# A new static step order for a chunked recurrent attention with an MLP: ones first on VectorE, some constants early, pads later

## The chip, the cores and the metric

One core of a Trainium2 chip. The metric is the time of one execution in microseconds (us). The kernel before took 266.17 us (median of three runs, 264.39 to 269.71). PE is TensorE, DVE is VectorE, ACT is ScalarE, POOL is GpSimd, SP is SyncE, which here only issues DMA.

## The reference, cut to what matters

A recurrent attention (4 batches, 8 heads, 768 steps, head size 40), whose output goes through an MLP with a squared ReLU (3072 tokens, 320 to 2048 to 320):

```python
for t in range(S):
    y[:, :, t] = einsum('bhd,bhde->bhe', rt, state)
    Sa = einsum('bhde,bhe->bhd', state, at)
    state = state * wt[:, :, None, :] - einsum('bhd,bhe->bhde', Sa, bt)
    state = state + einsum('bhd,bhe->bhde', vt, kt)
...
h = x @ w_in
g = maximum(h, 0)**2
return g @ w_out
```

## The kernel before

The recurrence is worked in chunks of 64 steps. There are 24 groups (12 chunks of two pairs of batches), and each group runs the same list of some sixty named steps. A list in the source gives one order for all steps of all groups; each engine runs its own steps of it in that order. `KBS1.2` is step KBS1 of group 2; `~3` is three warm-up matmuls on a tile of ones.

```python
ORDER = """
TBL.0 zK2.0 LWb.0 zL1.0 zR1.0 zS2.0 LWa.0 zV3.0 zR2.0 zU0.0 LKa.0 LWa.1 ...
... (cut)
"""
class Plan:
    def add(self, name, g, eng, dur, fn, deps=(), mode=None, alloc=None, frees=None, dma=None):
        ...   # keeps name, group, engine, function, deps; dur and dma are not kept
    def run(self):
        for t in ORDER.split(): ...   # checks the deps, gives out PSUM buffers, returns the functions in that order
...
def load(name, dst, step, src, other, deps):     # four buffers for each kind
    eng = "ACT" if g == 0 and name in ("LK", "LB") else "POOL" if g >= AQ and name == "LA" else "SP"
    for be in range(2): ... q_.dma_start(out=..., in_=tok(src, b0 + be))
    ...
load("LW", wf, 0, w, False, lambda be: [("LN", g - NL)])
load("LK", kbf, 320, k, True, lambda be: [(f"KBS{be}", g - NL)])
load("LB", kbf, 320, b, False, lambda be: [(f"KBS{be}", g - NL)])
...
add("LN", g, "ACT", 0.47, f, [..., ("LWa", g), ("LWb", g), ...])
add(f"KBS{be}", g, *(("DVE", 0.47) if g < 3 and be else ("POOL", 0.87)), f, [..., ("LK" + "ab"[be], g), ("LB" + "ab"[be], g), ("EXN", g), ...])
...   # from group 6 on KB is transposed by a DMA in SyncE's queue:
add("KX", g, "SP", 1.25, f, [("KBS0", g), ("KBS1", g), ("EB", g - NK)], dma=(40, 0.036, 0.1 + late, 1.0))
...   # the output's store, also in SyncE's queue
add("OST", g, "SP", 0.6, f, [("OE", g)], dma=(5, 0.088, 1.15, 0.9))
```

The chain of a group is: LW (load of w, SyncE), LN (its logarithm, ACT), LO (GpSimd), CS and CE (cumulative sums, PE), exponentials (ACT), KBS (GpSimd; VectorE for the first three groups' second half) and AS (GpSimd), then transposes and matmuls. SyncE's queue holds the loads of w, k and b (but for k and b of group 0, which ACT issues), the first loads of a, the transposes KX and the stores OST, 190 entries in one file: an entry that waits holds up all behind it. From the sixth on each also waits on one of eight semaphores in turn (in the trace of the kernel before 23 to 25 entries are on each), so that at most eight are under way. GpSimd issues the loads of v and r, and those of a from group 4 on, between its own computing.

Of the kernel before, what the change touches and what calls it, by code (L numbers as in the profile page):

```python
# [8 lines left out]
BF16 = mybir.dt.bfloat16  # L9
# [6 lines left out]
TBL.0 zK2.0 LWb.0 zL1.0 zR1.0 zS2.0 LWa.0 zV3.0 zR2.0 zU0.0 LKa.0 LWa.1 zA1.0 zS1.0 LKb.0 LWa.2 zF1.0 LBa.0 ones.0  # L16
zV1.0 UI.0 LAa.0 zF0.0 UE.0 LBb.0 ID.0 LWb.1 zL0.0 zF2.0 LN.0 LV1.0 SELB.0 LKb.1 TI.0 LO.0 zK0.0 LAb.0 zA0.0 zS0.0
LV0.0 ~10 CS.0 TE.0 LWb.2 zR0.0 EXN.0 I2.0 CE.0 LR.0 LAb.1 KBS1.0 KBS0.0 EXE.0 LAb.2 LN.1 zV0.0 ~3 KT.0 LR.1 LBa.1
AS.0 KTE.0 SEL.0 ~3 AT.0 wi1.0 LAa.1 MASK.0 LN.2 ATE.0 GLM.0 VC.0 LO.1 ~2 EB.0 LBb.1 EBE.0 LV0.1 ~1 CE.1 LKa.1 LO.2
EXE.1 zU1.0 LWb.3 ~1 XV.0 zK1.0 RT.0 LR.2 UB.0 zF3.0 LAa.2 LV1.1 UA.0 zV2.0 RTE.0 ~2 COR.0 wi2.0 CS.1 MA.0 LWa.3  # L20
CE.2 AS.1 MB.0 EXN.1 LKb.2 LV1.2 ~1 AT.1 VT.0 EXE.2 LAa.3 ATE.1 wj1.0 VTE.0 ST.0 KBS0.1 KBS1.1 CP.0 zR3.0 LBa.2
LV0.2 CPE.0 KT.1 LBb.2 wj2.0 LN.3 KTE.1 LKa.2 AS.2 ~2 CS.2 RT.1 EXN.2 STE.0 LAb.3 YC.0 wj0.0 RTE.1 EB.1 YE.0 LO.3
SX.0 VC.1 EBE.1 LKa.3 LR.3 CE.3 wi0.0 EXE.3 SXE.0 XV.1 LBa.3 LV1.3 wp0.0 AT.2 UA.1 RT.2 ATE.2 LKb.3 UB.1 KBS0.2 CS.3
wp1.0 RTE.2 COR.1 KBS1.2 LBb.3 XT.0 AS.3 MA.1 KT.2 XTE.0 MB.1 U1.0 wo0.0 KTE.2 EXN.3 VT.1 LV0.3 AT.3 VC.2 VTE.1 EB.2
UX1.0 GLM.1 GLM.2 EBE.2 UY1.0 LWb.4 ST.1 RL1.0 KBS0.3 LWa.4 STE.1 XV.2 X0.2 CP.1 LBb.4 UB.2 GLM.3 U0.0 CPE.1 KBS1.3
UA.2 UY0.0 LWa.5 UX0.0 wo1.0 KT.3 RL0.0 ATE.3 COR.2 KTE.3 YC.1 MA.2 YE.1 RT.3 MB.2 EB.3 SQ0.0 SX.1 RTE.3 LWb.5 XT.1
VT.2 XTE.1 LN.4 LKb.4 D0.0 EBE.3 VC.3 LO.4 ST.2 U0.1 LV0.4 SXE.1 CS.4 SQ1.0 D1.0 EXN.4 LAa.4 LBa.4 UX0.1 STE.2 LR.4
UY0.1 CE.4 VTE.2 RL0.1 LKa.4 XV.3 X0.3 CP.2 LWa.6 LN.5 U1.1 CPE.2 KBS1.4 UY1.1 EXE.4 LWa.7 UX1.1 UB.3 LAb.4 SX.2
LKb.5 RL1.1 SQ0.1 D2.0 LV1.4 SXE.2 D3.0 LWb.8 UA.3 LO.5 YC.2 OE.0 YS.2 LWb.6 KBS0.4 COR.3 YE.2 RT.4 LBa.7 D0.1 SQ1.1
RTE.4 LR.5 KT.4 LWb.7 MA.3 LV1.5 XT.2 D1.1 MB.3 XTE.2 AS.4 KTE.4 ST.3 LKa.5 VC.4 CS.5 LAb.5 U1.2 LBa.5 AT.4 LN.6  # L30
LAa.5 UX1.2 ATE.4 LBb.5 EXN.5 VT.3 LR.6 UY1.2 VTE.3 LV0.6 EB.4 RL1.2 OST.0 CE.5 EBE.4 LO.6 D2.1 LKa.7 EXE.5 LV0.5
RT.5 LN.7 STE.3 LBb.6 XV.4 KBS0.5 X0.4 U0.2 UB.4 CP.3 UA.4 D3.1 LAa.6 CPE.3 UX0.2 LKb.6 OE.1 KBS1.5 UY0.2 RTE.5
SQ1.2 SX.3 LAb.6 RL0.2 KT.5 LKa.6 SXE.3 CS.6 GLM.4 KTE.5 LBa.6 LO.7 COR.4 EXN.6 YC.3 SQ0.2 YS.3 LWa.8 AS.5 RT.6 MA.4
CS.7 YE.3 RTE.6 OST.1 D0.2 LV1.6 EXN.7 AT.5 XT.3 LWa.9 LV1.7 D1.2 ATE.5 VC.5 XTE.3 KBS1.6 EB.5 LKb.7 U0.3 MB.4 EBE.5
CE.6 LR.7 LWb.9 VT.4 LN.8 KBS0.6 D2.2 VTE.4 EXE.6 LBb.8 XV.5 LAa.7 X0.5 CP.4 UA.5 AS.6 D3.2 CPE.4 LBb.7 UB.5 UY0.3
OE.2 LO.8 KX.6 AT.6 VC.6 UX0.3 ATE.6 GLM.5 ST.4 LAb.7 RL0.3 YC.4 LKb.8 YS.4 LAb.8 COR.5 YE.4 CS.8 MA.5 LV1.8 U1.3
SQ0.3 LKa.9 MB.5 XT.4 UX1.3 KBS0.7 EXN.8 STE.4 UY1.3 VT.5 OST.2 LAa.8 RL1.3 XTE.4 D0.3 LWb.10 VTE.5 KBS1.7 EB.6
LBa.9 U0.4 SQ1.3 CE.7 LR.8 EBE.6 UY0.4 LN.9 LKb.9 UX0.4 EXE.7 LAb.9 D1.3 RL0.4 LWa.10 LO.9 SX.4 CP.5 SXE.4 GLM.6
ST.5 LV0.7 CPE.5 KX.7 RT.7 XV.6 AS.7 X0.6 D2.3 UA.6 SQ0.4 LV0.9 LKa.8 UB.6 D3.3 RTE.7 STE.5 U1.4 LR.9 LBa.8 CS.9
OE.3 LV1.9 COR.6 YC.5 MA.6 YS.5 LV0.8 UY1.4 YE.5 MB.6 UX1.4 KBS1.8 LKb.11 XT.5 SX.5 RL1.4 XTE.5 LKb.10 AT.7 SXE.5  # L40
CE.8 OST.3 SQ1.4 D0.4 EXE.8 VT.6 EXN.9 ATE.7 D1.4 LBb.9 LN.10 ST.6 VC.7 LO.10 LKa.11 U0.5 STE.6 EB.7 KBS0.8 LWb.11
UX0.5 EBE.7 D2.4 GLM.7 UY0.5 LAa.9 D3.4 VTE.6 RL0.5 KX.8 AS.8 RT.8 XV.7 LV0.10 X0.7 OE.4 SQ0.5 CP.6 U1.5 UA.7 OST.4
UY1.5 CPE.6 RTE.8 LWa.11 UX1.5 UB.7 AT.8 D0.5 RL1.5 ATE.8 SX.6 CS.10 SXE.6 LBb.12 YC.6 EXN.10 SQ1.5 COR.7 LWa.12
KBS0.9 YS.6 RT.9 MA.7 YE.6 D1.5 LWb.12 RTE.9 LAa.10 XT.6 D2.5 LBa.10 VC.8 XTE.6 KBS1.9 EB.8 MB.7 U0.6 EBE.8 LKa.10
LR.10 UY0.6 VT.7 GLM.8 LBb.10 LV1.10 UX0.6 VTE.7 D3.5 RL0.6 CE.9 KX.9 XV.8 OE.5 SQ0.6 X0.8 ST.7 EXE.9 CP.7 LN.11
STE.7 AS.9 OST.5 U1.6 UA.8 UY1.6 CPE.7 UB.8 LAb.10 UX1.6 LBb.11 D0.6 RL1.6 LO.11 AT.9 SX.7 ATE.9 LAb.11 LBa.11 CS.11
SQ1.6 LV1.11 YC.7 LWa.13 COR.8 YS.7 LV0.11 MA.8 D1.6 LWb.13 YE.7 MB.8 D2.6 LR.11 EXN.11 LWa.14 XT.7 KBS0.10 CE.10
XTE.7 VC.9 SXE.7 EB.9 U0.7 KBS1.10 EXE.10 EBE.9 ST.8 VC.10 VT.8 LAa.11 KX.10 UY0.7 LN.12 STE.8 D3.6 LV0.12 VTE.8
UX0.7 OE.6 AS.10 LWb.14 SX.8 RL0.7 RT.10 OST.6 SXE.8 LO.12 XV.9 X0.9 CP.8 UA.9 GLM.10 U1.7 LV1.12 CPE.8 RTE.10 UY1.7
UX1.7 LKb.14 UB.9 AT.10 RL1.7 LKb.12 CS.12 ATE.10 YC.8 SQ0.7 COR.9 LKa.12 KBS1.11 YS.8 RT.11 MA.9 YE.8 LBa.12 D0.7  # L50
EXN.12 KBS0.11 SQ1.7 XT.8 D1.7 MB.9 XTE.8 LAa.12 EB.10 LKb.13 VC.12 U0.8 EBE.10 GLM.9 UY0.8 LR.12 RTE.11 KX.11 UX0.8
CE.11 VT.9 LN.13 LBb.14 D2.7 VTE.9 EXE.11 LO.13 XV.10 RL0.8 LBb.13 X0.10 AS.11 ST.9 CP.9 STE.9 VC.11 U1.8 LAb.13
D3.7 UA.10 CPE.9 LAb.12 UY1.8 UB.10 SX.9 OE.7 LR.13 UX1.8 SQ0.8 OST.7 CS.13 RL1.8 LKa.14 SXE.9 YC.9 YS.9 COR.10
KBS1.12 LKa.13 YE.9 EXN.13 AT.11 D0.8 ATE.11 KBS0.12 MA.10 CE.12 XT.9 D1.8 LN.14 LAa.13 XTE.9 MB.10 SQ1.8 EB.11
LO.14 U0.9 EXE.12 UY0.9 EBE.11 KX.12 GLM.11 VT.10 LV1.13 UX0.9 LR.14 VTE.10 ST.10 LWa.15 AS.12 XV.11 STE.10 X0.11
LWa.16 CP.10 UB.11 D2.8 CPE.10 UA.11 AT.12 RL0.9 D3.8 LWb.15 COR.11 ATE.12 RT.12 LBa.13 MA.11 YC.10 YS.10 MB.11 U1.9
YE.10 CS.14 LKa.15 OE.8 SQ0.9 SX.10 EXN.14 OST.8 XT.10 UY1.9 XTE.10 UX1.9 LBa.15 VT.11 RL1.9 LBa.14 D0.9 KBS0.13
VTE.11 EB.12 LKa.16 U0.10 SQ1.9 LAa.14 CE.13 EBE.12 D1.9 LAb.14 EXE.13 LKb.15 UY0.10 LN.15 LV0.13 LWb.16 UX0.10
RTE.12 SXE.10 D2.9 KBS1.13 RL0.10 ST.11 AS.13 KX.13 XV.12 STE.11 X0.12 CP.11 UA.12 GLM.12 U1.10 LV0.15 CPE.11 D3.9
LBb.15 AT.13 LV1.14 OE.9 UY1.10 UB.12 ATE.13 UX1.10 OST.9 LO.15 SQ0.10 RT.13 RL1.10 COR.12 YC.11 LWb.18 YS.11  # L60
KBS0.14 CS.15 YE.11 RTE.13 D0.10 LWa.17 EXN.15 LAa.15 XT.11 SX.11 LBa.16 XTE.11 MA.12 KBS1.14 EB.13 U0.11 MB.12
EBE.13 CE.14 LV0.14 LWb.17 D1.10 LN.16 LAb.15 VT.12 SQ1.10 EXE.14 KX.14 UX0.11 VC.13 LO.16 VTE.12 UY0.11 LV1.15
D2.10 SXE.11 LKb.17 RL0.11 XV.13 AS.14 RT.14 LBb.16 ST.12 LR.15 X0.13 STE.12 U1.11 UA.13 CP.12 LR.16 UB.13 UY1.11
# [80 lines left out]
def kernel(  # L144
# [21 lines left out]

# [526 lines left out]
```

## Time and profile before

| | before |
|---|---|
| median of 3 | 266.17 us |
| span of the profiled run, mean granted clock | 264.9 us, 0.988 |
| PE busy | 92% |
| PE late against its pace (see the prediction) at 39 us / at the end | 20.7 / 27.3 us |

The prediction below shows the page, the sums by stretch and the start. The lines of the waits: who waited for what, us in total, times, longest.

```profile
POOL KB L331 <- DMA KBf<-in_b_dram: 6.9, 3, 5.0
ACT LNW L282 <- DMA Wf<-in_w_dram: 3.4, 1, 3.4
```

GpSimd's wait of 5.0 us (at 129 us) cost PE little: the only stop of PE near it is 0.9 us at 139 us, for the transpose of that KB.

### The profile page before, as it was taken

What the parts mean: (1) busy time and instruction counts of PE and PEld (TensorE: products, weight loads), DVE (VectorE), ACT (ScalarE), POOL (GpSimd) and SP (SyncE); (2) the same over time, 40 slices, a digit from 0 to 9 for tenths busy, and PEclk for the clock granted to TensorE, in tenths of its full rate; (3) what the DMA queues carried; (4) which work ended last, traced back from release to release, by engine and by line L of the source; (5) the groups of instructions that cost most, each with busy time, mean ns of one, the idle gap of its engine ahead of it and who ended that gap; (6) DMA issues with size and microseconds to landing.
All of it is one profiled execution on the core that took longest, in us unless ns stands there. A gap on an engine that the chain in (4) does not pass through costs nothing.

```text
span 264.9 us, 13096 instructions
## 1 busy us (share of the span) xinstructions
PE 243.5 (92%) x5809; PEld 193.8 (73%) x5809; DVE 180.1 (68%) x296; ACT 163.2 (62%) x289; POOL 162.3 (61%) x244
## 2 busy tenths in 40 slices
PE   4887979999999999999999999999999899999970
PEld 1345767877877788787877788888878688878750
DVE  7659976696856676768666668686767658786520
ACT  2344665687755757775675876578485675646340
POOL 3789728987975469567489758576967593400000
PEclk9979999999999999999999999999999999999997
DMA  7999999798799699789699879779899677200110
GB/s 117 156 180 169 202 199 167 137 155 155 141 143 136 127 132 161 145 141 144 106 135 152 169 120 169 131 133 139 138 113 142 110 131 102 66 25 16 32 36 26
DMA packets 111913, 33.75 MB, mean 127 GB/s; under 512 B 101232, under 2 KB 109808, under 8 KB 111856
## 3 DMA queue, kind: packets, MB, share of 16 engines
q1 hardware_dynamic: 100272, 20.79, 52.0%
q0 software_dynamic: 9472, 11.80, 25.2%
q8 instruction: 45, 0.74, 1.2%
q10 hardware_dynamic: 2112, 0.33, 0.8%
q14 instruction: 12, 0.10, 0.1%
HBM read 28.84 MB, written 3.93 MB: 124 GB/s over the span
## 4 chain that ended last, share of the span: by engine, by line
PE 74%; DMA 5%; ACT 2%; issue 2%; POOL 1%; DVE 0%; ACTq 0%; POOLq 0%
PE fo L569 19%; PE hp L551 15%; DMA KBT<-KB 5%; PE hp L542 4%; PE vt L488 4%; PE sx L476 3%; PE eb L405 2%; PE cs L298 2%; PE x L420 2%; PE cp L405 2%; PE y L502 2%; PE ce L311 2%; PE rt L376 2%; PE st L457 2%; PE x L442 2%; PE ar L369 2%
## 5 line engine op out<-in xcount | busy, mean ns | idle before, releaser
L556 ACT ACTIVATE RL<-hp 128x1024 bf16<-128x1024 f32 x46 | 47.1, 1023 | 32.7 <-PE hp L551 32.2
L569 PE MATMUL fo<-WOUT,GT 128*128 128x320 bf16 x384 | 65.5, 300 | 0.6 <-DVE GT L560 0.5
L331 POOL TENSOR_TENSOR KB<-KBf,EXN 128x320 bf16<-128x320 f32 x45 | 40.6, 909 | 36.9 <-PE y L502 21.4
L551 PE MATMUL hp<-XT,WIN 128*128 128x128 bf16 x736 | 51.7, 219 | 1.1 <-issue 1.0
L551 PEld LDWEIGHTS <-WIN 128*128 128x128 bf16 x768 | 44.9, 98 | 4.8 <-issue 1.7
L560 DVE TENSOR_TENSOR GT<-RL 128x1024 bf16<-128x1024 bf16 x48 | 37.8, 787 | 9.0 <-ACT RL L556 8.9
L569 PEld LDWEIGHTS <-GT 128*128 128x128 bf16 x384 | 33.0, 98 | 11.9 <-DVE GT L560 1.1
L409 DVE TENSOR_TENSOR CPM<-cp,MASK 128x1024 bf16<-128x1024 f32 x24 | 29.3, 1220 | 8.5 <-PE cp L405 8.5
L409 DVE TENSOR_TENSOR EBM<-eb,MASK 128x1024 bf16<-128x1024 f32 x24 | 29.3, 1221 | 7.6 <-PE eb L405 7.4
L343 POOL DMA_DIRECT2D Vf<-in_v_dram x48 | 33.9, 706 | 0.0
L290 POOL TENSOR_TENSOR LLO<-LNW 128x320 bf16<-128x320 f32 x24 | 18.4, 767 | 19.5 <-ACT LNW L282 15.2
L264 POOL DMA_DIRECT2D Af<-in_a_dram x40 | 28.2, 706 | 0.4 <-issue 0.4
L433 ACT ACTIVATE UZ<-x 64x320 bf16<-64x320 f32 x48 | 20.7, 431 | 9.7 <-PE x L428 8.1
L337 POOL TENSOR_TENSOR A<-Af,EXE 128x320 bf16<-128x320 f32 x24 | 21.2, 882 | 6.8 <-ACT EXE L320 2.3
L447 ACT ACTIVATE VM<-x 64x320 bf16<-64x320 f32 x48 | 20.6, 430 | 7.6 <-PE x L442 6.8
L304 ACT ACTIVATE EXN<-cs 128x640 f32<-128x640 f32 x24 | 16.9, 702 | 10.4 <-PE cs L298 8.7
L468 DVE TENSOR_TENSOR STB<-st,GLM 128x640 bf16<-128x640 f32 x22 | 18.0, 818 | 7.7 <-PE st L462 7.1
L515 DVE TENSOR_TENSOR YB<-y,EXE 128x320 bf16<-128x320 f32 x24 | 11.8, 490 | 13.5 <-PE y L510 12.0
L492 DVE COPY VMT<-vt 128x1024 bf16<-128x1024 bf16 x24 | 16.5, 686 | 4.4 <-PE vt L488 4.3
L282 ACT ACTIVATE LNW<-Wf 128x320 f32<-128x320 f32 x24 | 11.2, 468 | 12.8 <-PE ce L315 7.0
L542 PE MATMUL hp<-XT,WIN 64*128 64x128 bf16 x368 | 18.1, 217 | 0.0
L347 ACT ACTIVATE VM<-Vf 128x640 bf16<-128x640 f32 x24 | 17.5, 732 | 0.3 <-DMA Vf<-in_v_dram 0.2
(90 smaller groups left out, 454.6 us busy)
## 6 DMA issues: line engine op xcount, KB each, us to landing
Wf<-in_w_dram SPq DMA_DIRECT2D x48, 80.0 KB
Vf<-in_v_dram POOLq DMA_DIRECT2D x48, 80.0 KB, 5.2
out_dram<-OSB SPq DMA_DIRECT2D x24, 160.0 KB
KBf<-in_k_dram SPq DMA_DIRECT2D x46, 80.0 KB
KBf<-in_b_dram SPq DMA_DIRECT2D x46, 80.0 KB
Af<-in_a_dram POOLq DMA_DIRECT2D x40, 80.0 KB, 4.6
RB<-in_r_dram POOLq DMA_DIRECT2D x24, 80.0 KB, 4.8
WOUT<-in_moe_w_out_dram POOLq DMA_DIRECT2D x2, 640.0 KB, 9.2
```

The costliest lines, as they stand in the source:

```text
L264: q_.dma_start(out=V(dst, step * be, [(40, 8), (1, 40)], 64 * h, 64), in_=tok(src, b0 + be))
L331: (nc.vector if g < 3 and be else nc.gpsimd).tensor_tensor(out=V(kb, 512 * be, [(64, 8), (1, 40)]), in0=V(kbf, 320 * be, [(40, 8), (1, 40) ...
L337: nc.gpsimd.tensor_tensor(out=V(at, 0, [(64, 8), (1, 40)]), in0=V(af, 0, [(40, 8), (1, 40)]), in1=V(exe, 0, [(40, 8), (1, 40)]), op=ALU.mult)
L343: nc.gpsimd.dma_start(out=V(vf, 320 * be, [(40, 8), (1, 40)], 64 - 64 * be, 64), in_=tok(v, b0 + be))
L409: nc.vector.tensor_tensor(out=V(dst, 0, [(64, 16), (1, 64)]), in0=V(psum(key, g), 0, [(64, 16), (1, 64)]), in1=V(MASK, 0, [(0, 16), (1, 64 ...
L433: nc.scalar.activation(out=V(uz, 320 * be, [(1, 320)], 64 * be, 64), in_=V(psum("x", g), 0, [(1, 320)], 64 * be, 64), func=ACTF.Copy, scal ...
L447: nc.scalar.activation(out=V(vm, 512 * be, [(64, 8), (1, 40)], 64 * be, 64), in_=V(psum("x", g), 0, [(40, 8), (1, 40)], 64 * be, 64), func ...
L542: mm(out=V(p, 512 * s + 128 * i, [(1, 128)]), lhsT=wcol(1 + s, blk, 64 * s, 64), rhs=xt[64 * s:64 * s + 64, 128 + 128 * s:256 + 128 * s], ...
L551: mm(out=V(p, 512 * s + 128 * i, [(1, 128)]), lhsT=wcol(x, blk, 0, 128), rhs=xt[:, 128 * x:128 * x + 128], start=False, stop=i == 3 and x > 0)
L556: nc.scalar.activation(out=rl[:], in_=psum(hk, g)[:], func=ACTF.Relu)
L560: nc.vector.tensor_tensor(out=gt[:], in0=rl[:], in1=rl[:], op=ALU.mult)
L569: mm(out=p[:, 0:320], lhsT=gt[:, 512 * s + 128 * i:512 * s + 128 * i + 128], rhs=WOUT[:, DM * blk:DM * blk + DM], start=blk == 0, stop=blk ...
```

## The change

The intent: the ones go first on VectorE, so that the warm-up of PE can begin at once; the constants follow early; the zeroing of pad columns comes later; and the order of all steps is searched anew with new durations in the model of the search. On VectorE the search brought forward only part of the constants: MASK and SELB are its 6th and 2nd step (28th and 16th before), TI and TE its 18th and 22nd (17th and 21st before). The core of the diff (the list has 86 lines; cuts are marked):

```diff
 ORDER = """
-TBL.0 zK2.0 LWb.0 zL1.0 zR1.0 zS2.0 LWa.0 zV3.0 zR2.0 zU0.0 LKa.0 LWa.1 zA1.0 zS1.0 LKb.0 LWa.2 zF1.0 LBa.0 ones.0
-zV1.0 UI.0 LAa.0 zF0.0 UE.0 LBb.0 ID.0 LWb.1 zL0.0 zF2.0 LN.0 LV1.0 SELB.0 LKb.1 TI.0 LO.0 zK0.0 LAb.0 zA0.0 zS0.0
-LV0.0 ~10 CS.0 TE.0 ...
+TBL.0 ones.0 LWb.0 SELB.0 UE.0 UI.0 zS1.0 LWa.0 zL1.0 zV3.0 LKa.0 MASK.0 LAa.0 zK1.0 LBb.0 LKa.1 zU1.0 zK2.0 LKb.0
+zA1.0 zL0.0 LWa.1 zR0.0 zA0.0 LBa.0 zF0.0 LWb.1 LN.0 zR2.0 zK0.0 LV0.0 zV2.0 TI.0 LAb.0 LO.0 zF3.0 LAa.1 LV1.0 zV1.0
+~9 CS.0 ...
 ... (the rest of the 86 lines)
-                    add(..., 0.68, f, deps(be), dma=(20, 0.0224, 1.15 + late, 0.9))
+                    add(..., 0.68, f, deps(be), dma=(51, 0.008, 1.35, 0.9))
 ... (other durations and dma figures; none of them is emitted)
+    VDMA = (99, 99)
 ... (a branch for a transpose of VM by DMA, which this range switches off)
```

## The prediction

> **What bounds the kernel now.** I read the page first, then the sums over four stretches, then the waits of PE (TensorE), and last the first 35 us in order of time.
>
> ```profile
> span 264.9 us, 13096 instructions
> PE 243.5 (92%) x5809; PEld 193.8 (73%) x5809; DVE 180.1 (68%) x296; ACT 163.2 (62%) x289; POOL 162.3 (61%) x244
> PE   4887979999999999999999999999999899999970
> PEclk9979999999999999999999999999999999999997
> DMA  7999999798799699789699879779899677200110
> ...
> 0.00:8.00 8.00, 4.38 (x11) 1.35 (x12) 6.25 (x34) 1.75 (x2) 3.67 (x11) 1.00 0.76 120
> 8.00:38.70 30.70, 25.18 (x534) 17.26 (x534) 22.59 (x44) 16.95 (x33) 21.50 (x33) 0.94 1.17 182
> 38.70:249.00 210.30, 206.08 (x5180) 169.69 (x5180) 148.79 (x216) 140.55 (x250) 137.16 (x200) 1.00 0.79 127
> 249.00:265.00 16.00, 7.86 (x89) 5.46 (x86) 2.43 (x4) 3.95 (x5) 0.00 (x0) 0.90 0.10 31
> ...
> PE warm L660 <- DVE ones_b L594: 3.6, 1, 3.6
> PE eb L405 <- DMA KBT<-KB: 1.9, 2, 1.0
> PE x L442 <- issue: 1.5, 2, 1.3
> ```
>
> PE is the bound: 92% busy, and in the long third stretch 206.1 of 210.3 us. No other engine is over 68%. So the time is PE's work, plus what PE loses at the start, plus a few waits, plus a tail. In the rows of 40 slices the first six slices are the ragged ones; there the DMA row is full as well (1.17 from 8.0 to 38.7 us, 0.79 afterwards).
>
> To see where time is lost I gave each step of the order its pace: the mean distance from its start to the next step's start between 45 and 249 us, where PE had no idle time. A group of four 320-column matmuls takes 0.549 us, eight transposes 0.449, and so on. Where the next step uses the array in another way (128 rows at once, 64-row tiles, 64-column tiles) it takes 0.09 us more (X0, 0.144 before its like, 0.246 before another). From the first useful matmul on, this paces the program at 230.0 us. Against that pace PE is 8.0 us late when useful work begins, 20.7 at 39.2 us, 21.3 at 50, 24.4 at 148, 26.2 at 207 and 26.3 at 246. So of 26.3 us lost, 20.7 are lost before 39 us and 5.6 later. The later ones are waits for the two transposes by DMA (near 139 and 207 us) and stops in the middle of a run of matmuls with no releaser ("issue": 0.6 at 77, 0.5 at 109).
>
> The start in order of time:
>
> ```profile
> 3.39 0.17 DVE L594 MEMSET ones_b<- 128x128 bf16 x1
> 3.62 4.45 PE L660 MATMUL warm<-ones_b 128*128 128x512 bf16 x10 [3.62 <-DVE ones_b L594]
> 5.44 0.47 ACT L282 ACTIVATE LNW<-Wf 128x320 f32<-128x320 f32 x1 [3.35 <-DMA Wf<-in_w_dram]
> 6.00 0.71 POOL L290 TENSOR_TENSOR LLO<-LNW 128x320 bf16<-128x320 f32 x1 [0.78 <-ACT LNW L282]
> 6.95 0.38 DVE L592 COPY TI<-UI 64x64 bf16<-64x64 bf16 x1
> 8.00 0.45 PE L298 MATMUL cs<-LNW,TI 64*128 64x320 bf16 x2
> ...
> 12.03 0.72 DVE L621 COPY SEL<-ID 128x64 bf16<-128x64 bf16 x2
> 12.66 0.95 DVE L608 COPY MASK<-UE 64x64 bf16<-64x64 bf16 x2
> 13.64 0.42 DVE L381 COPY ART<-ar 128x512 bf16<-128x512 bf16 x1
> 14.13 0.41 PE L405 MATMUL eb<-ART,KBT 40*128 40x64 bf16 x16 [1.14 <-DVE ART L381]
> ...
> 32.60 0.86 POOL L331 TENSOR_TENSOR KB<-KBf,EXN 128x320 bf16<-128x320 f32 x1 [1.37 <-DMA KBf<-in_b_dram]
> ```
>
> The tile of ones is the eleventh thing on VectorE, so the ten warm-up matmuls begin at 3.62 and fill PE until 8.07; the first cumulative sum (cs) stands behind them. Its data were ready at 6.71 (LLO), its constant TI at 7.33. Later SEL and MASK are made on VectorE just when ART should be copied; eb waits 1.14 us for it.
>
> [...] ten warm matmuls from 3.62 take 4.45 us, three from 9.38 take 0.81; and the clock row has a 7 where PE had been idle at 10 to 14 us. [...] the two copies of TE take 0.36 us with GpSimd idle, the two of MASK 0.95 beside a GpSimd subtraction. [...] The 1.17 above is the sum of SyncE's and GpSimd's queues[...].
>
> **The change part by part.** Apart from the order list, nothing emitted changes: the new durations and DMA figures only feed the search, and the new branch for a transpose of VM by DMA is switched off (its range is 99 to 99). Each engine has the same number of instructions; 25 warm matmuls before, 25 after. So there are four things to price.
>
> (1) Ones first, 9 warm matmuls before cs instead of 10. Ones moves from 3.39 to about 0.95. The warm ones then run from 1.1 to about 5.0 (9 x 0.43) and are out of the way. By itself this frees PE, but cs still needs LLO at 6.71, which follows the landing of Wf at 5.4 (its two loads are first in both orders). On VectorE TI now stands behind about 4.5 us of memsets and MASK, so it starts at about 5.4 and ends by 6.5. Cs starts at about 6.8 for 8.0: 1.2 us.
>
> (2) Constants early. The KB product on GpSimd follows 1.2 us sooner; KBT is copied at 10.1 for 11.4; then one memset of 0.76, and ART at about 11.6 for 13.64, eb at about 12.1 for 14.13. So 2.0 us here, and the same for the first correction (15.6 for 17.7). All of it is on PE's path at this point.
>
> (3) What of these 2 us lasts to 39 us. The load that the fourth KB product waits for (KBf, at 32.6) is the 28th on SyncE in both orders. Each load waits for the landing of the one eight before it, and the DMA engines have no free share from 4 us on, so it can't land much earlier; a GpSimd queue that starts 2 us sooner may even push it back. The product ends at 33.47, and the transposes that need it (KT.3) ran at 34.68. With 2 us taken off, PE would want them at 32.7 and has to wait until about 33.5. So some 1.2 us last; I take 1.1.
>
> (4) The new order after that. Switches of array use fall from 220 to 210, eight of the ten after 39 us: 10 x 0.09 = 0.9 us. For the transposes by DMA I counted the paced PE work between the last KB product and eb. Before, the shortest is 6.0 us (chunk 13, which stalled 0.9); the stalls at 139 and 207 us took 6.1 and 6.9 us from issue to release. After, the shortest are 7.2, 7.6, 7.7 and 7.7, and chunk 13 has 11.2. I expect 1.9 us of stalls to become 1.0: 0.9 saved. The "issue" stops (about 3 us) are not tied to a dependence and should come back at other places: 0. The last 40 steps on PE are nearly the same list, so the 7.4 us from PE's end to the end of the span stay.
>
> Sum: 1.1 + 0.9 + 0.9 = 2.9 us off 266.2: 263.3 us.
>
> **The rivals.** First, the whole 2 us of the start last, because the loads land earlier too (SyncE's first loads are reordered, wj and wi go out 1 to 2 us sooner), and the stalls by DMA vanish: 2.0 + 0.9 + 1.9 = 4.8, 261.4 us. Against it speaks the full DMA row. Second, DMA alone sets the pace of the start: GpSimd's earlier weight loads take share from the KB loads, and KT.3 and the first fo (its weights landed at 36.97 and 42.65) come no earlier or later than now. Then only (4) is left, 264.4. For it speaks that the DMA share is over 1.0 in nearly all of the time up to 44 us. Third, an order searched by a model is tight where the model is wrong: the copies of A to ART have 1.5 us before eb in the lower quarter for 2.2 before, the move of chunk 7's transpose has 4.6 us to eb for 7.9. If eight such places cost 0.4 us each, (4) is eaten up: about 266.5. Fourth, PE idle between 5 and 6.8 us puts the clock back to half for longer; at the half clock the 10 us around it hold little PE work, so at most 1 us.
>
> **Range and chances.** Three runs of the kernel before spread from 264.4 to 269.7, so a single median is good to about 1 us. The parts above are uncertain by about 0.8, 0.8 and 1.0, and the stops by 1. Together about 2 us: range 260.3 to 266.3. Faster by over 2% means below 260.8, which needs rival one and luck: 0.13. Slower by over 2% needs stalls that nothing in the order shows: 0.02.
>
> **What would show it.** First warm matmul near 1.1 us, cs near 6.8, eb near 12.1: if not, (1) or (2) is wrong. The fourth KB product still held by its load at 31 to 33 us: (3). PE late by about 19.5 us at the first fo for 20.7. Waits of eb on KBT of about 1 us in all for 1.9. PE busy should fall by about 1 us plus the change in clock. It is wrong if PE's first 39 us end more than 2.5 us earlier (then the start was not held by DMA), or if PE shows new waits on VectorE or ScalarE after 50 us.

## More of the kernel before

ACT's one wait for w, 3.4 us, is that of the very first load. In 23 groups after it no logarithm waited for its data.

## The result, and the profile after

| | before | after |
|---|---|---|
| median, same rounds (4 runs each) | 267.6 us (264.39 to 269.71) | 278.23 us (276.09 to 279.06) |
| ratio of fast runs | | 1.048, 95% interval 1.036 to 1.059 |
| span, clock of the profiled run | 264.9 us, 0.988 | 277.4 us, 0.964 |

A ratio here is the mean time of one kernel's fast runs over that of the other's fast runs of the same rounds, so it is not quite the ratio of the medians that I quote; "slow" is a run over 1.5% above the fastest of its kernel. The kernel after is slower by 3 to 5%: measured a second time it came out at 1.030 (e13, 1.022 to 1.038). Much of that difference lies in which runs count as fast: by the medians of all runs the two are 1.040 and 1.034. So ratios of different calls that differ by under 0.02 are not told apart below. Both sign and size of the prediction were wrong. All runs gave correct results.

The page and the sums by stretch of the kernel after, to be held against the first fence of the prediction (in the sums: stretch, its length, busy us and instructions of PE, PEld, DVE, ACT, POOL, then granted clock, DMA share, GB/s):

```profile
span 277.4 us, 13090 instructions
PE 247.6 (89%) x5809; PEld 197.6 (71%) x5809; DVE 179.4 (65%) x296; ACT 163.7 (59%) x289; POOL 161.9 (58%) x244
PEclk9799599999997999999998999999999999999998
...
0.00:8.00 8.00, 5.00 (x15) 1.64 (x16) 6.05 (x37) 2.10 (x3) 2.99 (x10) 1.00 0.78 113
8.00:38.70 30.70, 24.32 (x476) 17.52 (x478) 20.47 (x37) 14.91 (x29) 21.80 (x34) 0.83 1.09 172
38.70:249.00 210.30, 197.93 (x4967) 162.74 (x4961) 141.89 (x208) 136.07 (x243) 137.06 (x201) 0.98 0.83 127
249.00:278.00 29.00, 20.35 (x365) 15.75 (x363) 10.96 (x16) 10.57 (x17) 0.00 (x0) 0.94 0.09 28
```

The loss is in the third stretch: PE is busy 197.9 of the 210.3 us in which it had been busy 206.1, and the work left over is done behind 249 us, where PE now has 20.4 us of work for 7.9. PE's busy time grew by 4.1 us, which fits its longer time at half clock (mean 0.83 for 0.94 in the second stretch, 0.98 for 1.00 in the third); VectorE's, ACT's and GpSimd's changed by 0.7 or less. For the rest PE waits; the waits say for what (first PE's own, then those of other engines for loads):

```profile
PE cs L299 <- POOL LLO L291: 3.2, 2, 2.7
PE kt L356 <- DVE SB L482: 3.0, 1, 3.0
PE cp L406 <- issue: 1.6, 1, 1.6
...
ACT LNW L283 <- DMA Wf<-in_w_dram: 10.7, 9, 3.9
POOL A L338 <- DMA Af<-in_a_dram: 5.3, 2, 3.6
POOL KB L332 <- DMA KBf<-in_k_dram: 4.9, 1, 4.9
```

ACT waits for w nine times where it had waited once (the longest, 3.9 us, is again the very first load; the longest of the new ones is 3.1); GpSimd waits 4.9 us for one load of k. The page's median from issue to landing of such loads (80 KB each) is:

```profile
Wf<-in_w_dram SPq DMA_DIRECT2D x48, 80.0 KB, 5.8
KBf<-in_b_dram SPq DMA_DIRECT2D x46, 80.0 KB, 6.2
```

How one such wait reaches PE, three lines of the kernel after in order of time (start, length, engine, line, what; in brackets how long the engine stood idle before it and who released it):

```profile
72.53 1.54 SPq L265 DMA_DIRECT2D KBf<-in_k_dram  x1
...
80.70 0.89 POOL L332 TENSOR_TENSOR KB<-KBf,EXN 128x320 bf16<-128x320 f32 x1 [4.95 <-DMA KBf<-in_k_dram]
...
83.21 0.31 PE L299 MATMUL cs<-LLO,TI 64*128 64x320 bf16 x2 [2.72 <-POOL LLO L291]
```

The load LKa.7 is issued at 72.53, lands at 80.57, and GpSimd, which runs its steps in order, stands still until then. LO.9 comes behind it on GpSimd, though it has nothing to do with that load, and CS.9 on PE waits 2.7 us for LO.9. In SyncE's queue LKa.7 stands behind LWa.12, which nothing needs until group 12.

I measured PE's lateness against the pace of the prediction in every trace. The columns are the lateness in us at eb of group 0 (13 us), at the first fo (D0.0, about 39 us), at D0.6 (about 98 us) and at the end; the growth in the two long stretches; and the sum of PE's stops over 0.3 us behind 98 us that nothing released ("issue"). The "12 us" and "6 us" are the lead given to loads, explained at e6. One profiled run each, fast ones but for e6 and e13, which were counted slow (over 1.5% above the fastest of their kernel):

| kernel | eb.0 | D0.0 | D0.6 | end | D0.0 to D0.6 | D0.6 to end | issue stops |
|---|---|---|---|---|---|---|---|
| before | 12.5 | 20.7 | 22.7 | 27.3 | 2.0 | 4.6 | 0.5 |
| after | 11.1 | 22.6 | 30.3 | 40.7 | 7.7 | 10.4 | 4.6 |
| after again (e13) | 11.2 | 22.2 | 30.3 | 41.4 | 8.1 | 11.1 | 5.7 |
| e3, before + constants first | 12.6 | 19.7 | 23.6 | 27.2 | 3.9 | 3.6 | 1.6 |
| e4, after + KBS1.2 moved | 12.1 | 18.9 | 28.4 | 38.0 | 9.5 | 9.6 | 4.2 |
| e6, e4 + queue sorted, 12 us | 11.5 | 22.1 | 23.5 | 34.6 | 1.4 | 11.1 | 5.3 |
| e12, after + queue sorted, 12 us | 11.4 | 18.5 | 20.7 | 30.9 | 2.2 | 10.2 | 4.3 |
| e14, the same again | 11.4 | 21.1 | 23.9 | 32.2 | 2.8 | 8.3 | 2.0 |
| e15, after + queue sorted, 6 us | 11.2 | 18.7 | 26.7 | 34.8 | 8.0 | 8.1 | 4.5 |
| e17, e14 + 54 instructions in front | 12.0 | 18.8 | 21.5 | 31.6 | 2.7 | 10.1 | 5.0 |
| e18, e14 + 150 instructions in front | 11.2 | 23.2 | 25.7 | 31.0 | 2.5 | 5.3 | 2.0 |

The paced work itself is 0.9 us shorter after (fewer switches of how the array is used). So the 12.5 us between the two spans are 13.4 of lateness less 0.9, and the 13.4 are 1.9 up to 39 us, 5.7 between 39 and 98 us and 5.8 behind 98 us. The experiments are about these three numbers. The middle one repeats well: 7.7 and 8.1 in the two profiles of the kernel after, 2.2 to 2.8 in the four of the sorted order e12. The first does not (18.5 to 23.2 us at 39 us), and the last varies by 2 us in the same program (e12, e14).

The start of the kernel after, in order of time:

```profile
6.50 0.32 PE L299 MATMUL cs<-LNW,TI 64*128 64x320 bf16 x2 [1.39 <-ACT LNW L283]
7.30 0.31 PE L299 MATMUL cs<-LLO,TI 64*128 64x320 bf16 x2 [0.49 <-POOL LLO L291]
12.72 0.41 PE L406 MATMUL eb<-ART,KBT 40*128 40x64 bf16 x16
...
28.20 0.83 DVE L332 TENSOR_TENSOR KB<-KBf,EXN 128x320 bf16<-128x320 f32 x1 [3.75 <-DMA KBf<-in_k_dram]
...
30.91 1.01 PE L356 MATMUL kt<-ID,KB 128*128 128x128 bf16 x8 [3.02 <-DVE SB L482]
```

The early part does what it should: cs at 6.50 for 8.00, eb at 12.72 for 14.13. At XV.1 (24 us) PE is 15.6 us late for 17.9. Then VectorE, whose new order has KBS1.2 ahead of the weight copies, the copy of sx and others, waits 3.75 us for a load of k, and PE waits 3.0 us for what is behind it. Then the granted clock falls to half for most of a slice (the 5 in the row above; from 28.9 to 35.7 us in the record). The record of the clock begins with the first change to full, at 9.2 us before, 4.95 after, 13.5 in e4; until then the warm-up matmuls came every 0.43 us, afterwards, at the full clock, every 0.21, and the means above count that time as full.

### The profile page after: what moved, and what is told of

Same layout as the page of the kernel before. It is cut to its first block, busy times and chain, and to the rows that moved or that the text cites.

```text
span 277.4 us, 13090 instructions
## 1 busy us (share of the span) xinstructions
PE 247.6 (89%) x5809; PEld 197.6 (71%) x5809; DVE 179.4 (65%) x296; ACT 163.7 (59%) x289; POOL 161.9 (58%) x244
## 4 chain that ended last, share of the span: by engine, by line
PE 71%; DMA 9%; SPq 7%; issue 5%; DVE 3%; POOL 3%; ACT 1%; POOLq 0%; DVEq 0%
PE fo L575 17%; PE hp L557 15%; SPq L265 7%; DMA KBf<-in_k_dram 6%; PE hp L548 4%; PE vt L490 4%; DMA Wf<-in_w_dram 3%; PE sx L477 3%; PE eb L406 3%; PE cp L406 2%; PE y L508 2%; PE x L421 2%; PE st L458 2%; PE ce L312 2%; PE rt L377 2%
## 5 line engine op out<-in xcount | busy, mean ns | idle before, releaser
L562 ACT ACTIVATE RL<-hp 128x1024 bf16<-128x1024 f32 x46 | 47.0, 1021 | 28.9 <-PE hp L557 24.9
L332 POOL TENSOR_TENSOR KB<-KBf,EXN 128x320 bf16<-128x320 f32 x45 | 40.1, 899 | 33.3 <-PE y L508 22.1
L557 PE MATMUL hp<-XT,WIN 128*128 128x128 bf16 x736 | 54.7, 225 | 0.3 <-issue 0.2
L557 PEld LDWEIGHTS <-WIN 128*128 128x128 bf16 x768 | 47.2, 101 | 4.7 <-issue 1.0
L575 PEld LDWEIGHTS <-GT 128*128 128x128 bf16 x384 | 33.7, 99 | 13.1 <-DVE GT L566 2.4
L338 POOL TENSOR_TENSOR A<-Af,EXE 128x320 bf16<-128x320 f32 x24 | 22.4, 935 | 17.4 <-ACT EXE L321 5.6
L305 ACT ACTIVATE EXN<-cs 128x640 f32<-128x640 f32 x24 | 16.8, 702 | 10.2 <-PE cs L299 7.7
L386 ACT ACTIVATE ART<-rt 128x512 bf16<-128x512 f32 x24 | 14.2, 593 | 9.3 <-PE rt L377 9.0
L283 ACT ACTIVATE LNW<-Wf 128x320 f32<-128x320 f32 x24 | 11.2, 467 | 13.7 <-DMA Wf<-in_w_dram 10.7
L548 PE MATMUL hp<-XT,WIN 64*128 64x128 bf16 x368 | 18.5, 220 | 0.9 <-ACT RL L562 0.9
```

Of the source, the lines that this page charges most:

```text
L332: (nc.vector if g < 3 and be else nc.gpsimd).tensor_tensor(out=V(kb, 512 * be, [(64, 8), (1, 40)]), in0=V(kbf, 320 * be, [(40, 8), (1, 40) ...
L338: nc.gpsimd.tensor_tensor(out=V(at, 0, [(64, 8), (1, 40)]), in0=V(af, 0, [(40, 8), (1, 40)]), in1=V(exe, 0, [(40, 8), (1, 40)]), op=ALU.mult)
L548: mm(out=V(p, 512 * s + 128 * i, [(1, 128)]), lhsT=wcol(1 + s, blk, 64 * s, 64), rhs=xt[64 * s:64 * s + 64, 128 + 128 * s:256 + 128 * s], ...
L557: mm(out=V(p, 512 * s + 128 * i, [(1, 128)]), lhsT=wcol(x, blk, 0, 128), rhs=xt[:, 128 * x:128 * x + 128], start=False, stop=i == 3 and x > 0)
L562: nc.scalar.activation(out=rl[:], in_=psum(hk, g)[:], func=ACTF.Relu)
L575: mm(out=p[:, 0:320], lhsT=gt[:, 512 * s + 128 * i:512 * s + 128 * i + 128], rhs=WOUT[:, DM * blk:DM * blk + DM], start=blk == 0, stop=blk ...
```

## The experiments

Each call ran beside the kernel before on the same chip: e1 to e4 (its median 265.74), e5 to e8 (269.61), e9 to e12 (269.96), e13 to e16 (268.18), e17 and e18 (267.98). My first theory: the new order puts loads in SyncE's queue where they come late (late loads). First rival: the new order of the matmuls is itself too tight. "Queue" below means SyncE's queue; nothing else moves unless said.

| run | median us | ratio | 95% interval |
|---|---|---|---|
| e1 after, queue of before | 272.87 | 1.025 | 1.016 to 1.034 |
| e2 before, queue of after | 288.81 | 1.082 | 1.071 to 1.092 |
| e3 before, constants first | 266.98 | 1.001 | 0.992 to 1.010 |
| e4 after, KBS1.2 moved | 277.02 | 1.037 | 1.025 to 1.048 |
| e5 e4, two loads forward | 274.29 | 1.012 | 1.002 to 1.022 |
| e6 e4, queue sorted, 12 us | 271.62 | 1.003 | 0.994 to 1.011 |
| e7 e4, queue and GpSimd of before | 292.96 | 1.089 | 1.082 to 1.097 |
| e8 e3, one transpose forward | 268.01 | 0.994 | 0.987 to 1.001 |
| e9 e4, queue sorted, 6 us | 274.58 | none | |
| e10 e4, queue sorted, 16 us | 273.58 | 1.026 | 1.014 to 1.038 |
| e11 e3, queue sorted, 12 us | 269.64 | 1.012 | 1.001 to 1.023 |
| e12 after, queue sorted, 12 us | 266.89 | 1.005 | 0.996 to 1.014 |
| e13 after again | 277.31 | 1.030 | 1.022 to 1.038 |
| e14 e12 again | 270.57 | 1.012 | 1.006 to 1.019 |
| e15 after, queue sorted, 6 us | 276.18 | 1.029 | 1.022 to 1.037 |
| e16 e12, transposes forward | 271.91 | 1.019 | 1.012 to 1.025 |
| e17 e14, 9 warm matmuls cut in four | 272.77 | 1.015 | 1.009 to 1.021 |
| e18 e14, 25 warm matmuls cut in four | 268.10 | 1.002 | 0.996 to 1.007 |

In e9 to e12 four of the seven runs of the kernel before were over 1.5% above its fastest, so that the ratio rests on its three quickest (265.1 to 266.2); by the medians of all runs those four stand at 1.017, 1.013, 0.999 and 0.989. I use these ratios with care.

**e1 and e2: the whole queue exchanged.** The queue as the other kernel has it, all other engines as they were. A stretch of it, from the entry OST.1 on:

```diff
 kernel after, SyncE's sequence (cut)
-OST.1 LBb.7 LKb.7 LWb.9 LWb.8 LBb.8 LKa.8 LWa.9 LKb.8 KX.6 OST.2 LBa.7 LWa.12 LKa.7 ...
+OST.1 LWa.9 LKb.7 LWb.9 LBb.8 LBb.7 KX.6 LKb.8 LKa.9 OST.2 LWb.10 LBa.9 LKb.9 LWa.10 KX.7 LKa.8 ...
```

> The changed kernel, with SyncE's own queue (the loads of w, k, b, the first of a, the transposes by DMA, the stores) put back in the order of the kernel before; the four other engines keep the new order. Theory 1 (the new order issues loads too close to their use, and engines that work in order stand behind them): most of the 11 us come back, 264 to 270 us; GpSimd's KB product of chunk 7 no longer waits some 5 us for its load, and VectorE's KB product of chunk 2 no longer some 3.7. Theory 2 (the loss is PE's own stops inside groups of matmuls and the half clock after them): stays over 274 us. Theory 3 (the new order on the compute engines is too tight by itself): over 274 us too, but with the waits on loads gone.

> The mirror: the kernel before, with SyncE's queue in the new order. Theory 1: slower than before by 4 us or more, 271 to 279 us, with waits of GpSimd, ScalarE or VectorE on loads of k and w. Theories 2 and 3: within 2 us of before.

The queue of before takes the kernel after from 1.048 to 1.025; the queue of after takes the kernel before from 1 to 1.082. In e2 the waits show where (its profiled run was counted slow, 291.6 us; its three fast runs took 285.9 to 289.0):

```profile
ACT LNW L281 <- DMA Wf<-in_w_dram: 31.0, 11, 4.8
```

So the queue alone can cost far more than the whole change did, and more than the 271 to 279 us that I had expected. But e1 keeps half of the loss (272.9 us, between the ranges of the theories): a queue fits the order that it was made with, and neither exchange is a clean test. Put in the columns of the table above, the kept traces part it better: between 39 and 98 us the lateness grew by 3.2 us in e1 (7.7 after) and by 12.8 in e2 (2.0 before); what e1 keeps is behind 98 us, 10.1.

**e3: constants first, alone.** VectorE's head rewritten in the kernel before (ones, then constants, then pads):

```diff
-zK2.0 zL1.0 zR1.0 zS2.0 zV3.0 zR2.0 zU0.0 zA1.0 zS1.0 zF1.0 ones.0 zV1.0 zF0.0 zL0.0 zF2.0 SELB.0 TI.0 ...
+ones.0 zL0.0 zR0.0 TI.0 TE.0 SEL.0 I2.0 MASK.0 SELB.0 zK0.0 zA0.0 zV0.0 zF0.0 zL1.0 ...
```

> The kernel before with one part of the change alone: on VectorE the tile of ones first, the constants TI, TE, SEL, I2 and MASK next, and the pads later, each ahead of its first use; all else in the order before. The prediction's steps 1 to 3: cs near 6.8 us for 8.0, eb near 12.3 for 14.1, and of these 2 us about 1.1 left at the first fo: 1 us faster than before. A rival (the loads set the pace of the start entirely): the same as before within 0.5 us although eb is early.

Cs came at 6.89 us. Eb stayed at 14.18, as AS.0 waited for a load of a that landed at 11.75. At the first fo PE was 1.0 us less late than before (19.7 for 20.7), the size of step (3) of the prediction, but not by its way, as eb was not earlier. The kernel before had a stop of 1.3 us without a releaser at 35.5 to 36.8 us that e3 had not, and e8 and e11, with the same VectorE order, are 21.7 and 18.7 us late there. So this one profile shows no gain that the constants made. Later PE lost time:

```profile
PE eb L404 <- DMA KBT<-KB: 2.9, 1, 2.9
```

The transpose KX.6 was issued at 65.34, behind two loads, 2.8 us after its KB was done, and landed 7.0 us later. Ratio 1.001.

**e4: KBS1.2 moved back on VectorE.**

```diff
 kernel after, VectorE's sequence (cut)
-... EBE.1 XTE.0 KBS1.2 wp1.0 SXE.0 ATE.2 wp0.0 KTE.2 ...
+... EBE.1 XTE.0 wp1.0 SXE.0 ATE.2 wp0.0 KBS1.2 KTE.2 ...
```

> The changed kernel with one step moved: VectorE's KB product of chunk 2 behind both copies of weights, as in the kernel before, and not ahead of them. If the start's loss is this one product holding VectorE while its load is under way, PE is no longer idle for 3 us before the transposes of chunk 2, and the time falls by 2 to 4 us to 274 to 276. If the loads are late for everything there, it falls by under 1 us.

In the profile the clock stays full from 13.5 to 39 us and PE is 18.9 us late at the first fo for 22.6. The time moved from 1.048 to 1.037, with intervals that overlap: the 2 to 4 us expected are not shown. The rest of the loss is unchanged: 9.5 us between 39 and 98 us.

**e5: one urgent load forward.** On e4:

```diff
-OST.1 LBb.7 LKb.7 LWb.9 LWb.8 LBb.8 LKa.8 LWa.9 LKb.8 KX.6 OST.2 LBa.7 LWa.12 LKa.7 ...
+OST.1 LBb.7 LKb.7 LBa.7 LKa.7 LWb.9 LWb.8 LBb.8 LKa.8 LWa.9 LKb.8 KX.6 OST.2 LWa.12 ...
```

> Base is the order after with KBS1.2 moved back (e4, ratio 1.037 to before, about 275 us of span). One edit more: the two loads LBa.7 and LKa.7 stand ahead of LWb.9 in SyncE's queue, where they stood behind KX.6, OST.2 and LWa.12. Theory 'late loads' (a load that comes late stops GpSimd, and the stop is carried to the end): GpSimd's wait of 4.9 us for KBf of k goes, CS.9 is no longer late (2.8 us), the half clock after it goes (1.3 us), and the whole ends 3 to 4 us earlier, ratio about 1.023 to 1.028. Rival 'the order of the matmuls is tight': another wait takes the place within two groups and the ratio stays within 0.005 of 1.037. Wrong for both: a longer time.

CS.9 no longer waits, and the profiled span fell from 274.7 to 271.4, by 3.3 us as expected; the ratio fell further than expected, to 1.012, but on two fast runs only. Between 39 and 98 us the lateness grew by 5.9 us for 9.5 in e4: the chain load, GpSimd, LO, CS is shown. That the whole span fell by as much is in part chance, as e5 lost 1.8 us more than e4 before 39 us and 1.5 less behind 98.

**e6 and e7: the whole queue sorted, or taken from before with GpSimd's.** For e6 I sorted the queue of e4 by a rule: a load 12 us of PE work ahead of its use (or 1.5 us after its buffer is free, if that is later), a transpose 2 us after its KB, a store 1.5 us after its output:

```diff
-OST.1 LBb.7 LKb.7 LWb.9 LWb.8 LBb.8 LKa.8 LWa.9 LKb.8 KX.6 OST.2 LBa.7 LWa.12 LKa.7 ...
+LBb.7 LKb.7 OST.1 LBa.7 LKa.7 LWb.9 LWa.9 KX.6 LBb.8 LKb.8 LKa.8 LBa.8 OST.2 LWa.10 LWb.10 KX.7 ...
```

e7 keeps the compute order of e4 on PE, VectorE and ACT, and takes the whole sequences of SyncE and of GpSimd from before.

> Base e4 again. All steps of SyncE's queue, and no other engine's, sorted anew: a load 12 us of PE work ahead of its use (or 1.5 us after its buffer is free, where that is later), a transpose of KB 2 us after its KB, a store 1.5 us after its output. Theory 'late loads': ACT's waits for Wf (14.9 us in e4), GpSimd's for KBf and the stops of CS.9, U1.6, AT.9 go; lag gained after 39 us falls from 19.0 to that of before (6.6) plus the unchanged issue stops and GpSimd's own loads (about 3); about 264 to 267 us, ratio 0.995 to 1.005. Rival 'the order of the matmuls is tight' (steps of PE too close behind the VectorE and ACT steps that feed them): at least 271, ratio over 1.02, with PE's stops now ended by VectorE, ACT or GpSimd steps that wait for no transfer.

> Base e4, with SyncE's and GpSimd's own sequences both taken whole from the kernel before, so that every load stands in its queue as before; PE, VectorE and ACT keep the new order. Theory 'late loads': since it is the distance from a load's place to its use that counts, and the uses now come by PE's new order, most of the loss goes: 266 to 269, ratio 1.00 to 1.012. Rival 'the order of the matmuls is tight': 271 or more as in e1 (1.025).

e6 came out as the theory said, 1.003. Its profiled run was slow, so I read from it only that between 39 and 98 us the lateness grew by 1.4 us for 9.5 in e4. e7 is a miss for the theory, 1.089: GpSimd's steps in the order of before stop ACT, VectorE and PE of the new order, for instance

```profile
ACT VM L347 <- DMA Vf<-in_v_dram: 21.9, 4, 8.2
```

as GpSimd issues those loads of v between its own steps. GpSimd's order belongs to PE's order; I can't use it as a test of the loads.

**e8: e3 with one transpose forward.** SyncE: `LWb.9 LBb.8 LBb.7 KX.6` became `LWb.9 LBb.7 KX.6 LBb.8`.

> The order before with ones and constants first on VectorE (e3, ratio 1.001) and one edit more: the transpose KX.6 stands ahead of LBb.8 in SyncE's queue, and LBb.7 ahead of it. In e3 KX.6 was issued 2.8 us after its KB was done, behind those two, landed 7 us later, and EB.6 stopped PE for 2.9 us, which ate the 1.0 us won at the start. Theory 'a gain at the start lasts where the queue has no late transfer': that stop goes, the lag at the end is 1 to 2.5 us less than in e3: 263 to 265, ratio 0.990 to 0.997. Rival 'the gain is swallowed at the next transfer whatever one does, as the transfers set the pace': another transfer stops PE in the next 20 us, ratio 0.999 to 1.003.

EB.6 did not stop. Ratio 0.994, 0.987 to 1.001: in the expected range, and the lowest ratio, but not told apart from the kernel before. In its profile the lateness at the end was no smaller (28.7), as the start lost 2.7 us at a KB product; so I can't claim that the start's gain was kept.

**e9 to e12: the lead of the loads, and the two parts apart.** e9 and e10 are e6 with 6 and 16 us for 12; e11 is e3 with the sorted queue; e12 is the kernel after with the sorted queue alone, KBS1.2 left where it was.

```diff
 the rule's one number, and the base
-key = max(ready + 1.5, need - 12)     e6, e11 (on e3), e12 (on after)
+key = max(ready + 1.5, need - 6)      e9
+key = max(ready + 1.5, need - 16)     e10
```

> As e6 (e4 with SyncE's queue sorted by need), but a load stands only 6 us of PE work ahead of its use in place of 12: the same rule, the same engines' orders, one number changed. In e6 the shortest time from a load's issue to its use was 7.1 us; here it should be some 4 to 7 us, near the 4.4 to 6.2 us that a load takes to land in the kernel after. Theory 'late loads': ACT and GpSimd wait for Wf and KBf again (over 15 us together on ACT LNW and POOL KB), ratio 1.02 to 1.05. Rival 'what helped in e6 was that the stores and transposes no longer stand ahead of loads, not how early the loads stand': ratio as e6, 1.00 to 1.01.

> As e6 with 16 us in place of 12. Theory 'late loads': e6 had taken the lateness away, so nothing more is to be won: ratio 0.995 to 1.008, as e6 within its interval. Rival 'still earlier loads win on': ratio under 0.99.

> The order before with constants first (e3, ratio 1.001), SyncE's queue sorted by the rule of e6 at 12 us: the candidate to beat both, since it has the early start and no load behind one that is needed over 10 us later (26 such loads in e3). Theory 'late loads': e3's stops for transfers go (EB.6 2.9 us, KBf), ratio 0.985 to 0.995. Rival 'before's loads were timely enough, the lag grows by stops that no transfer causes': 0.995 to 1.003. If KX or the stores now hold up the loads: slower than 1.003.

> The kernel after itself with SyncE's queue alone sorted by the rule of e6 at 12 us; KBS1.2 stays where the new order has it on VectorE. It parts the two causes: if they add up, the ratio is e6 plus what KBS1.2 cost (1.0476 - 1.0366 = 0.011), about 1.010 to 1.018. Rival 'KBS1.2 only hurt because its load LKb.2 came late in the queue': the sort of the queue moves nothing before g = 4 by much, so LKb.2 still lands at about 28 us and VectorE still stops; if it does not stop, 1.00 to 1.006.

e12 is the clean one: 266.89 against 269.96 by the medians, 1.005 by the ratio. e9 was slower than e12 by 7.7 us in the median, but three of its four runs were counted slow and it has no ratio; in its profile, a slow run too, the waits of ACT for w and of GpSimd for k were 29.6 us together, as forecast. e12 had been expected at 1.010 to 1.018 if the two causes add up; it is nearer to the rival, but its interval reaches both. e10 missed: 1.026, with a new wait of 3.2 us of EB.6 for KBT. With the loads earlier, KX.6 stands behind more of them. e11 missed too: four such waits for KBT, 6.7 us together. So loads can stand too early as well, where they hold up the transposes. KBS1.2, in e12 at the place where it had cost 3.75 us, waited 1.4 us, and in e14 and e16 nothing, although the first thirty entries of the queue are the same in these three as in the kernel after. In e18, with the same entries, it waited 3.4 us. What makes that one load later or earlier is not settled; the lateness at 39 us ranges from 18.5 to 23.2 us among kernels with the same first thirty entries (e12 and e18). In the traces of the new order it goes with the clock: 18.5 to 19.1 us in the five with no half clock between 13.7 us and the first fo (e4, e9, e12, e15, e17), 20.9 to 22.6 in the five with 6.8 to 10.2 us of it (after, e13, e6, e14, e16). Which is cause and which effect no run parts.

**e13 to e16: on one chip.** The kernel after, e12 again, e12 with 6 us for 12, and e12 with the transposes 0.3 us behind their KB for 2 (it moves KX.8, KX.11 and KX.17 two or three entries forward).

> The kernel after itself, so that it stands on one chip beside its own version with the sorted queue: ratio 1.03 to 1.05, as when it was first measured (1.048). Under 1.02 would mean that its loss belongs to the chip and not to the order.

> e12 again beside the kernel after: the same instructions on every engine, SyncE's queue alone in another order. Theory 'the loss is made in SyncE's queue': 0.995 to 1.010, at least 2.5% under e13. If the lead that the new order has at 39 us (about 2 us) lasts, under 0.995. Rival 'e12 was lucky': over 1.015.

> e14 with the loads 6 us of PE work ahead of their use in place of 12 (e9 without the move of KBS1.2; e9 gave no ratio, as three of its four runs were counted slow). Theory 'how early a load stands counts': ACT and GpSimd wait for Wf and KBf 20 us or more together, ratio 1.015 to 1.04, between e14 and e13. Rival 'only the order among the loads counts' (no load behind one that is needed later): as e14 within 0.006.

> e14 with the transpose of KB 0.3 us after its KB in the rule in place of 2 us: it moves three places ahead for g = 8, two for g = 11 and 17, nothing else. The candidate to beat both. EB.11's stop of 1.6 us for KBT in e12 goes; 1 to 2 us less than e14, ratio 0.99 to 1.005. Rival 'the stop moves to the next transfer': as e14 within 0.004; if the transpose now holds the loads behind it, over e14.

By the means of the fast runs the kernel after took 274.9 us, with the sorted queue 270.3, with the queue sorted at 6 us 274.8, the kernel before 266.9. So on one chip the queue alone gives back 4.6 of the 8.0 us. The waits of e14, then of e15:

```profile
ACT LNW L282 <- DMA Wf<-in_w_dram: 7.3, 3, 4.1
POOL KB L331 <- DMA KBf<-in_k_dram: 1.4, 1, 1.4
```

```profile
ACT LNW L282 <- DMA Wf<-in_w_dram: 15.9, 9, 3.9
POOL KB L331 <- DMA KBf<-in_k_dram: 12.4, 6, 4.3
```

One number of the rule brings the nine waits of the kernel after back, and the 8.0 us between 39 and 98 us with them (2.8 in e14). In e15 no load of groups 4 and later stands behind one that is needed later; so it is not the order among the loads alone that counts but how early each is issued. From the traces, for groups 4 on: the first quartile of the time from the issue of a load of w to its logarithm is 10.8 us before, 7.1 after, 10.9 in e14 and 5.9 in e15. I had expected e14 to be 1.010 at most and 2.5% under e13; it was 1.012 and 1.7% under (270.3 for 274.9), and what is left over is the stretch behind 98 us. e16 was not faster but, if anything, slower (1.019), and EB.11 still waited, 2.7 us for 2.4 in e14. The theory missed; the rival is not shown either, as the stop stayed where it was.

**e17 and e18: the stops with no releaser.** Behind 98 us the sorted versions still lose 8 to 11 us for 4.6 before. In all of these but e14 the stops that nothing released make up the largest share. I numbered PE's instructions (weight loads and matmuls) in order of time: in all traces these stops, from 40 us on, fall on places 181 to 187 modulo 256 (87 stops over 0.3 us in the 20 traces). e17 and e18 leave the order as in e14 and lengthen the stream's head:

```diff
-    mm(out=warm[:], lhsT=ones_b[:], rhs=V(ones_b, 0, [(0, 4), (1, 128)]), start=True, stop=True)
+    for q in range(4):     # e17: the first 9 warm matmuls; e18: all 25
+        mm(out=warm[:, 128 * q:128 * q + 128], lhsT=ones_b[:], rhs=ones_b[:], start=True, stop=True)
```

> e14 with each of the first nine warm matmuls of 512 columns cut into four of 128: 54 instructions more at the head of PE's stream, every later step 54 places further on, and nothing else. In e12 and e14 PE stopped with no releaser at AT.9, YC.13 and SX.13, at places 183 to 187 of a count by 256, as all such stops over 0.45 us in all traces so far. Theory 'instructions are fetched 256 at a time': the stops come again at 183 to 187 modulo 256, so 54 places earlier in the order, at other steps, and their sum after 98 us (4.7 and 2.4 us in e12 and e14) changes by chance, 0.5 to 6. Rival 'these steps wait for something': AT.9, YC.13, SX.13 stop again, at places 54 further on modulo 256. The time as e14 (1.012) within 0.012 either way.

> As e17 with all 25 warm matmuls cut into four: 150 instructions more. Same theories: fetch 183 to 187 modulo 256 again; the time as e14 within 0.012 and, if the places of the stops matter, not the same as e17: a sum of stops under 2 us after 98 us should go with a ratio under 1.008, one over 4 us with a ratio over 1.012.

The seven stops over 0.3 us in the two runs from 40 us on came at places where earlier traces had stopped, to the instruction (1211, 3003, 5305, 6327, twice 7095, 8887). So they came at other steps: in e12 place 7095 was in SX.13 (1.65 us). Now it is in eb in e17 (1.8 us), and in st in e18 (2.0 of the 3.0 us). The lines of e12, e17 and e18:

```profile
PE sx L476 <- issue: 1.7, 1, 1.7
```

```profile
PE eb L405 <- issue: 1.8, 1, 1.8
```

```profile
PE st L462 <- issue: 3.0, 2, 2.0
```

The stops belong to the places in the stream, not to the steps. How long they are varies: in the same program they came to 4.3 us (e12) and 2.0 (e14). e17 with 5.0 us of them behind 98 us took 1.015, e18 with 2.0 us 1.002, as I had written before; but e12 and e14 go against that rule (4.3 us with 1.005, 2.0 with 1.012), and the two profiled runs of e17 and e18 took nearly the same time (269.96 and 269.35 us), as e18 lost 4.4 us more before 39 us. So what the stops cost in the mean times is not shown by the ratios. Within one trace they can be added up. Behind 98 us the kernel after loses 5.8 us more than before: 4.1 of it are these stops (4.6 for 0.5); 1.6, an estimate by the pace, are the half clock from 144.9 to 148.3 us that follows the stop of 1.6 us ending at 144.8; waits for GpSimd's product A add 1.9 (of these 0.9 at 107 us behind a load of w that ACT had waited 3.1 us for), and 1.9 of waits for transposes are gone.

## Why the prediction was wrong

- **Step (1), ones first**: right for the start of cs. The warm-up began at 1.12 us and cs at 6.50 for 6.8 predicted; its second half waited for LLO until 7.30. The fourth rival came as said: PE idled from 5.1 to 6.5 us, and the clock was back at half from 8.4 to 11.8.
- **Step (2), constants early**: mostly right. Eb at 12.72 for 12.1 predicted and 14.13 before: 1.4 us for 2.0; the first correction at 15.85 for 15.6 predicted and 17.73 before.
- **Step (3), 1.1 us last to 39 us**: not confirmed. Where VectorE's head alone was changed, e3's 1.0 us came without an early eb, by luck as far as the traces tell. In the kernel after the named load did not hold the fourth KB product at all (it began at 33.70 us without a wait), and PE was 1.9 us later against its pace at the first fo than before: VectorE waited 3.75 us for the load of KBS1.2, and the clock fell to half. The step looked at one load on GpSimd and not at VectorE's new order. But that wait comes and goes with the same queue, so this term is not settled by times, and the second rival (DMA alone sets the pace of the start) is neither shown nor refuted.
- **Step (4), the new order**: this is the step that failed. It had two terms and lacked a third. The 0.9 us of fewer switches are in the paced work, and the waits for transposes did shrink (0.8 us of eb on KBT for 1.9). The term "the 'issue' stops ... should come back at other places: 0" had it right that they come at other steps, and the size wrong: 4.6 us behind 98 us for 0.5. And there was no term for the loads. I had counted the PE work between KB and eb, and between A's product and its copy, but not that between the issue of a load and its use. It would have shown: 10.8 us to 7.1 in the first quartile for w, with loads that take 4.4 to 6.2 us to land and can wait in a file first. The runs put 5.7 us there (between 39 and 98 us), which e12, e14 and e6 take away and e15 brings back. The prediction's own sign of error came: PE waited 0.9 us for VectorE at 62 us and 0.9 for ACT at 103 us. It had given a slowdown of over 2% a chance of 0.02, as one that "nothing in the order shows"; the order did show the loads.
- **Third rival** ("an order searched by a model is tight where the model is wrong") was the right mechanism with the wrong places and size. I gave it eight places at 0.4 us and looked at compute steps; single stops of PE behind late loads cost 2.7 and 3.0 us, because GpSimd and VectorE hold everything behind them.
- **What stays open**: why the stops with no releaser are longer and more frequent with the new order (the traces show that the last packet of the instruction queue before a stop starts late, 1.9 us ahead for 3.7 elsewhere, not why), and the change of 4 us at the start from run to run. That the stops are those of instruction fetch is inferred from the places and the packets (last section), not shown by an experiment on the fetch. No version beat the kernel before by an amount that its interval shows; e8 came nearest (0.994).

## What to carry to other kernels

When a static order is exchanged, go through the in-order queues first: for each load count the time between its issue and its use, before and after, and hold it against the measured time from issue to landing. A load that is late can cost much where an in-order engine waits for it with unrelated work behind it (2.7 us of PE for GpSimd's 4.9 here, 0.9 for 5.0 in the kernel before); loads that are too early hold up the transposes behind them in the queue (3.2 us of EB.6 in e10, four waits of 6.7 us together in e11). And two orders of the same steps also differ in which steps fall on the places of the instruction stream where PE stops with no releaser (181 to 187 modulo 256 here); these stops made up 4.1 of the 5.8 us lost behind 98 us, and they can be tested by adding a few harmless instructions at the head.

## Loads and stops, as the traces show them

- GpSimd's loads of v, 80 KB each, took 5.2 us from issue to landing (before) and 5.0 (after; medians of the pages) with the DMA share at 0.79 and 0.83 (38.7 to 249 us); SyncE's of w, k and b, 80 KB too, took 4.4 to 6.2 (medians of the page after), a single one 8.0 us (LKa.7). The time from issue to landing with many loads under way is the one that a schedule needs.
- The instruction queue that fits PE (q8 of the page) moved 45 packets in 0.74 MB for PE's 11,618 instructions, which makes an estimated 258 instructions a packet; in e18 it moved 46 for 11,768. All 87 stops without a releaser (over 0.3 us, from 40 us on) lie at places 181 to 187 modulo 256.
- PE passed most of these places without a stop, but 87 in 20 traces stopped it for 0.3 to 2.8 us, up to 5.7 us in a run behind 98 us. Where PE did not stop, the last packet of that queue had begun 3.7 us ahead of the place (median of all traces), where it stopped 1.9 us ahead of the stop (middle half 1.4 to 2.3).
- The step at which such a stop falls moves with the length of the stream: place 7095 lay in sx in e12, and in eb and st with 54 and 150 instructions more at the head. These two took 1.015 and 1.002, with intervals just apart (1.009 to 1.021, 0.996 to 1.007); against the order without them (1.005 and 1.012) neither is told apart.
